# Attention with a gated feed-forward on one core: the end of the raw maxima with one transposition over 1,024 columns and three copies between partitions

## The chip, the cores and the metric

The kernel runs on one core of a Trainium2 chip. The metric is the time of one execution on the device in microseconds (us), as the median of several executions. Five engines work side by side: PE (matrix multiplications; PEld are its weight loads), DVE (vector), ACT (scalar functions), POOL (a second, slower vector engine) and SP, which here only issues transfers.

## The reference

Everything is in float32. `x` has 2,048 tokens of 448 numbers. `a` is attention with 16 heads of 28, `b` a feed-forward with 1,792 hidden units, and a gate of one number per token mixes them.

```python
q, k, v = split(x @ wqkv)                   # 16 heads of 28
p = softmax(q @ k.T * 28 ** -0.5)           # 2048 x 2048 for each head
a = (p @ v) @ wo
gate = x @ W_gate
b = (gate * (gate > 0) * (x @ W_up)) @ W_down
g = sigmoid((x * gate_w).sum(-1))
out = g * a + (1 - g) * b
```

## The kernel before

**Rounds.** Keys lie on partitions, queries along the columns. A head has 16 blocks of 128 keys; a round takes 8 of them, so 16 heads make 32 rounds of some 25 us each. In a round PE makes scores for 8 blocks of keys by 2,048 queries (`scores`, L323, and `raw_scores`, L330), maxima for the next head (`smax`, L292), a piece of the feed-forward (`gu_mm`, L716), and last the product of the probabilities with the values (`pv`, L753: 64 matmuls as PE runs them). What stands where is written by hand in the strings of `ROUNDS`, a letter for each step: s scores, r and q raw scores, d `raw_max`, m `smax`, x a feed-forward matmul, e an exponential, T the end of the raw maxima. Each engine runs its own queue in the order in which the code issues.

**Two ways to keep the exponential in bounds.** For half of the queries (column chunks 0 and 1) the maximum is known ahead and is subtracted within the matmul; ACT writes exp(score) at once (L325). For the other half (chunks 2 and 3, 1,024 queries) the scores of a round are copied out raw (L334 on ACT, L332 on DVE), one round ahead, and DVE keeps a running maximum over the 8 blocks of keys in `run(0)` and `run(1)`, each 128 partitions by 512 columns, next to each other in one tile (`raw_max`, L337; the tile is slot 8 and has the name P in the profile, as all the probability slots do).

**The end of the raw maxima** (`raw_top`, T in the strings, once in each of 31 rounds) makes one maximum for each of the 1,024 queries over the 128 partitions, all on DVE. It transposes the running maxima in blocks of 32 by 32 (L345), takes the maximum over the 32 columns of each block into `best_of`, 128 partitions by 32 (L348), copies the four groups of 32 partitions side by side on partitions 0 to 31 (`four`, L342; a copy is written as a maximum over one element), takes the maximum of the four (`square`, L351), transposes that back (L353) into a row of `rows2`, and in odd rounds also takes the maximum with the row of the round before (L356), again into `best_of`.

**What follows it.** SP writes the row to DRAM (L359, `mr_d`) and reads it back spread over all 128 partitions into the upper half of slot 8 (L366). In the next round POOL subtracts it from 8 blocks of raw scores (`raw_less`, L371, in the last round on DVE), ACT takes the exponentials (L375), and `pv` reads them. In odd rounds POOL also makes the difference of the two rows (L361). `raw_top` stands a few steps ahead of the end of a round, and `pv` comes last. Behind the end, DVE has the products of the feed-forward (L731), the copy or sum of what `pv` made (`os`, L757 and L759), and the maxima of the next round (L294), which give score banks back to PE.

**Where tiles lie.** `rows2` and `best_of` are in a pool that also holds the small tiles of `smax`; the pools with V, the first K and Q and the probability slots lie behind it.

Of the kernel before, what the change touches and what calls it, by code (L numbers as in the profile page):

```python
# [9 lines left out]
F32 = mybir.dt.float32  # L10
# [9 lines left out]
P = 128  # L20
# [109 lines left out]
def gated_mix_kernel(ctx, tc, x, wq, wo, wgu, wd, out):  # L130
    nc = tc.nc
# [5 lines left out]
    keep = ctx.enter_context(tc.tile_pool(name="keep", bufs=1))  # L137
# [88 lines left out]
    def slot(k):  # L226
        if k not in slots:
            slots[k] = p_slot((0, 1, 2, 3, 5, 6, 7, 4, 8)[k], f"P_{k}")
        return slots[k]
# [14 lines left out]
    def run(a, n=1):  # L244
        return slot(8)[:, a:a + n].rearrange("p a t -> p (a t)")
# [3 lines left out]

    rows2 = keep.tile([32, 2, 32], F32, name="rows2")  # L250
    row_a, row_b = rows2[:, 0], rows2[:, 1]
    best_of = keep.tile([P, 32], F32, name="best_of")

    Q = {}

# [83 lines left out]
    def raw_top(r):  # L339

        def copy(o, i):
            nc.vector.tensor_reduce(o, i.rearrange("p (a b) -> p a b", b=1), axis=AX.X, op=OP.max)  # L342

        for a in range(2):
            nc.vector.transpose(run(a), run(a))  # L345
        best, small = best_of, run(0)
        four, square = small[:32, :128].rearrange("p (a b) -> p a b", a=4), small[:32, 128:160]
        nc.vector.tensor_reduce(best, run(0, 2).rearrange("p (b i) -> p b i", i=32), axis=AX.X, op=OP.max)  # L348
        for a in range(4):
            copy(four[:, a], best[32 * a:32 * a + 32])  # L350
        nc.vector.tensor_reduce(square, four.rearrange("p a b -> p b a"), axis=AX.X, op=OP.max)  # L351
        row = row_b if r % 2 else row_a
        nc.vector.transpose(row, square)  # L353
        if r % 2:
            row = best_of[:32]
            nc.vector.tensor_reduce(row, rows2.rearrange("p a b -> p b a"), axis=AX.X, op=OP.max)  # L356

        def send():
            nc.sync.dma_start(mr_d[r], row)  # L359
            if r % 2:  # L360
                nc.gpsimd.tensor_tensor(row_a, row_a, row, op=OP.subtract)  # L361

        return send
# [469 lines left out]
    for r, order in enumerate(ROUNDS):  # L833
# [22 lines left out]
        for n, o in enumerate(steps):  # L856
# [3 lines left out]
            b = int(o[1]) if o[1:] else None  # L860
# [17 lines left out]
            elif o == "T":  # L878
                assert not new and not tops
                send = raw_top(r + 1)  # L880
                if not behind:
                    send()
# [50 lines left out]
        if not topped:  # L933
            raw_top(r + 1)()
# [214 lines left out]
```

## Time and profile before

| | |
|---|---|
| median of 3 executions | 1149.65 us (1149.62 to 1153.59) |
| the profiled execution | 1148.84 us, its span 1147.1 us |
| busy PE, PEld | 1142.2 us, 821.9 us |
| busy DVE, ACT, POOL | 919.6, 869.6, 705.6 us |
| granted clock of PE | 1.000 |

The span runs from the first to the last instruction of the profiled execution. In the views, a row of a group gives line, engine, operation, what is written from what is read, the shape and the count, then busy time and the mean of one in ns, then the idle time of the engine before it and who ended that. A row of a timeline gives start and duration in us, then the same; a bracket holds the idle time ahead and its releaser. "b" is the whole of PSUM, whose eight banks take what PE makes. Releasers are inferred: of several events that an instruction could wait for, the one named is the last that came.

### The profile page before, as it was taken

How to read it: one execution, taken by the hardware profiler on the slowest of the kernel's cores; microseconds unless marked ns; L12 is line 12 of the kernel's file. 1: busy time of each engine (PE TensorE's matmuls, PEld its weight loads, DVE VectorE, ACT ScalarE, POOL GpSimd, SP SyncE). 2: the span in 40 equal slices, each digit the busy share in tenths (PEclk: the TensorE clock that was granted, in tenths of full speed). 3: DMA queues.
4: the chain of work that ended last, by engine and by line, in shares of the span. 5: the costliest groups of instructions: out<-in, count | busy, mean ns of one | idle time of the engine just before them, and what ended most of it. 6: DMA issues, size and time to landing. Idle time of an engine off the chain costs nothing.

```text
span 1147.1 us, 18485 instructions
## 1 busy us (share of the span) xinstructions
PE 1142.2 (100%) x6188; PEld 821.9 (72%) x6188; DVE 919.6 (80%) x1615; ACT 869.6 (76%) x1544; POOL 705.6 (62%) x426
## 2 busy tenths in 40 slices
PE   9999999999999999999999999999999999999998
PEld 6888866666666666666666666666666666999997
DVE  6487488888899999999889999999999866544342
ACT  5311789999989999999989989999988977422221
POOL 5333368999987777878767877787887770000000
PEclk9999999999999999999999999999999999999999
DMA  9957855655664344543644354456433374654332
GB/s 315 349 193 267 310 186 183 219 195 178 204 201 144 127 153 167 176 144 125 228 145 145 115 163 153 154 175 200 140 124 121 115 252 166 209 169 131 103 106 79
DMA packets 74796, 201.50 MB, mean 176 GB/s; under 512 B 17130, under 2 KB 23746, under 8 KB 70274
## 3 DMA queue, kind: packets, MB, share of 16 engines
q1 hardware_dynamic: 67292, 171.89, 46.1%
q0 software_dynamic: 6976, 27.93, 6.7%
q8 instruction: 49, 0.80, 0.3%
q10 hardware_dynamic: 432, 0.49, 0.1%
q14 instruction: 47, 0.39, 0.1%
HBM read 139.63 MB, written 61.17 MB: 175 GB/s over the span
## 4 chain that ended last, share of the span: by engine, by line
PE 100%; DVE 0%; issue 0%
PE b L716 24%; PE b L753 20%; PE b L1053 12%; PE b L323 11%; PE b L292 11%; PE b L330 10%; PE b L524 6%; PE b L542 3%; PE b L1012 3%; PE b L572 0%; PE b L306 0%; PE b L513 0%; PE b L518 0%; DVE y L1059 0%; PE b L517 0%; DVE V L568 0%
## 5 line engine op out<-in xcount | busy, mean ns | idle before, releaser
L716 PE MATMUL b<-X,wg 128*128 128x512 f32 (+1 forms) x1232 | 389.7, 395 | 0.0
L294 DVE TENSOR_REDUCE mx<-b 128x1 f32<-128x512 f32 x528 | 339.2, 679 | 17.2 <-PE b L292 16.7
L371 POOL TENSOR_TENSOR P<-P,P 128x1024 f32<-128x1024 f32 x120 | 284.5, 2417 | 66.0 <-DMA P<-mr_d 41.3
L325 ACT ACTIVATE P<-b 128x512 f32<-128x512 f32 x528 | 301.1, 638 | 31.6 <-PE b L323 30.7
L371 POOL TENSOR_TENSOR V<-V,P 128x1024 f32<-128x1024 f32 x120 | 284.4, 2415 | 52.8 <-DMA P<-mr_d 38.1
L716 PEld LDWEIGHTS b<-X,wg 128*128 128x128 f32 (+1 forms) x1232 | 218.9, 187 | 56.7 <-issue 12.9
L337 DVE TENSOR_TENSOR P<-b,P 128x512 f32<-128x512 f32 x402 | 254.7, 681 | 1.8 <-ACT V L334 0.6
L753 PE MATMUL b<-P,v 128*32 128x512 f32 x1536 | 226.1, 594 | 0.0
L323 PE MATMUL b<-Q,K 128*128 128x512 f32 x528 | 199.3, 393 | 0.0
L292 PE MATMUL b<-K,Q 128*128 128x512 f32 x528 | 198.2, 392 | 0.0
L330 PE MATMUL b<-Q,K 128*128 128x512 f32 x496 | 184.7, 391 | 0.0
L753 PEld LDWEIGHTS b<-P,v 128*32 128x32 f32 x1536 | 60.1, 110 | 144.6 <-issue 138.4
L334 ACT ACTIVATE V<-b 128x512 f32<-128x512 f32 x239 | 137.9, 650 | 8.4 <-PE b L330 6.4
L1053 PE MATMUL b<-WD,hh 128*128 128x448 f32 x672 | 137.7, 365 | 0.0
L1053 PEld LDWEIGHTS b<-WD,hh 128*128 128x128 f32 x672 | 126.1, 188 | 10.2 <-DVE hh L189 0.2
L375 ACT ACTIVATE V<-V 128x1024 f32<-128x1024 f32 x128 | 129.4, 1113 | 1.3 <-POOL V L371 1.3
L334 ACT ACTIVATE P<-b 128x512 f32<-128x512 f32 x221 | 126.9, 645 | 3.7 <-PE b L330 1.7
L323 PEld LDWEIGHTS b<-Q,K 128*128 128x128 f32 x528 | 99.1, 188 | 30.5 <-DVE rl L731 6.7
L375 ACT ACTIVATE P<-P 128x1024 f32<-128x1024 f32 x120 | 118.1, 1071 | 0.0
L183 ACT ACTIVATE hh<-hr 128x512 fp32r<-128x512 f32 x52 | 32.8, 632 | 111.9 <-PE b L1053 111.7
L292 PEld LDWEIGHTS b<-K,Q 128*128 128x128 f32 x528 | 98.9, 188 | 20.9 <-DVE rl L731 0.8
L753 PE MATMUL b<-V,v 128*32 128x512 f32 x512 | 113.2, 594 | 0.0
(104 smaller groups left out, 1043.9 us busy)
## 6 DMA issues: line engine op xcount, KB each, us to landing
wg<-wgs_d SPq DMA_DIRECT2D x42, 896.0 KB
P<-mr_d SPq DMA_DIRECT2D x31, 512.0 KB
K<-qk_d SPq DMA_DIRECT2D x64, 224.0 KB
Q<-qk_d SPq DMA_DIRECT2D x64, 224.0 KB
h_d<-rl SPq DMA_DIRECT2D x56, 256.0 KB
hr<-h_d SPq DMA_DIRECT2D x52, 256.0 KB
wgs_d<-wg SPq DMA_DIRECT2D x14, 896.0 KB
qk_d<-st POOLq DMA_DIRECT2D x21, 512.0 KB, 5.5
```

Of the source, the lines that this page charges most:

```text
L292: nc.tensor.matmul(ps, Q[h][:, u * P:(u + 1) * P], K[h % 3][:, c * TB:(c + 1) * TB], start=True, stop=True)
L294: nc.vector.tensor_reduce(MX[h][:, k:k + 1], ps, axis=AX.X, op=OP.max)
L323: nc.tensor.matmul(ps, K[h % 3][:, kt * P:(kt + 1) * P], Q[h][:, j * TB:(j + 1) * TB], start=True, stop=True)
L325: nc.scalar.activation(prob(i, j), ps, AF.Exp, scale=SCALE)
L330: nc.tensor.matmul(ps, K[h % 3][:, kt * P:(kt + 1) * P], Q[h][:, j * TB:(j + 1) * TB], start=True, stop=True)
L334: nc.scalar.activation(prob(i, j), ps, AF.Copy)
L337: nc.vector.tensor_tensor(run(j - 2), ps, run(j - 2) if i % 8 > 1 else prob(i - 1, j), op=OP.max)
L371: engine.tensor_tensor(own, own, top(), op=OP.subtract)
L375: nc.scalar.activation(own, own, AF.Exp, scale=SCALE)
L716: nc.tensor.matmul(ps, WS[i][rows, s, a], xf(i // NF, b)[rows], start=(n == 0), stop=(n == NT - 1))
L753: nc.tensor.matmul(po[32 * j:32 * j + 32], VH[h][:, i % NK], prob(i, j), start=(i == i0), stop=(i == i0 + ni - 1))
L1053: nc.tensor.matmul(ACC[i // NF][t][:, :D], HH[i][:, a, t * P:(t + 1) * P], WD[:, f, b], start=(f == 0 and n == 0), stop=(f == NF - 1 and n ...
```

## The change

The two transpositions of 512 columns become one of 1,024 over `run(0, 2)`, which is the same memory. `best_of` grows from 32 to 128 columns, and `four` now lies in it, on partitions 0 to 31; the maxima of those partitions are already in its first 32 columns, so the first of the four copies is not needed. `square` is now in the first 32 columns of `run(0)`. In odd rounds the last maximum goes to the first 32 columns of `best_of`, as before. In the changed kernel the lines from L345 on have a number lower by one.

```diff
-    best_of = keep.tile([P, 32], F32, name="best_of")
+    best_of = keep.tile([P, 4 * 32], F32, name="best_of")
...
-        for a in range(2):
-            nc.vector.transpose(run(a), run(a))
-        best, small = best_of, run(0)
-        four, square = small[:32, :128].rearrange("p (a b) -> p a b", a=4), small[:32, 128:160]
+        nc.vector.transpose(run(0, 2), run(0, 2))
+        four, square = best_of[:32].rearrange("p (a b) -> p a b", a=4), run(0)[:32, :32]
+        best = best_of[:, :32]
         nc.vector.tensor_reduce(best, run(0, 2).rearrange("p (b i) -> p b i", i=32), axis=AX.X, op=OP.max)
-        for a in range(4):
+        for a in range(1, 4):
             copy(four[:, a], best[32 * a:32 * a + 32])
         nc.vector.tensor_reduce(square, four.rearrange("p a b -> p b a"), axis=AX.X, op=OP.max)
         row = row_b if r % 2 else row_a
         nc.vector.transpose(row, square)
         if r % 2:
-            row = best_of[:32]
+            row = best_of[:32, :32]
```

On DVE, the first end of the raw maxima, before (P_1234 is slot 8, in brackets whose events an instruction waits for):

```order
L345 STREAM_TRANSPOSE P_1234<-P_1234 128x512 [waits DVE_49] x2
L348 TENSOR_REDUCE best_of<-P_1234 128x32 [waits DVE_49]
L342 TENSOR_REDUCE P_1234<-best_of 32x32 [waits DVE_49]
L342 TENSOR_REDUCE P_1234<-best_of 32x32 x3
L351 TENSOR_REDUCE P_1234<-P_1234 32x32 [waits DVE_49]
L353 STREAM_TRANSPOSE rows_172<-P_1234 32x32 [waits DVE_49]
L356 TENSOR_REDUCE best_of<-rows_172 32x32 [waits DVE_49]
```

The same place now:

```order
L344 STREAM_TRANSPOSE P_1234<-P_1234 128x1024 [waits DVE_49]
L347 TENSOR_REDUCE best_of<-P_1234 128x32 [waits DVE_49]
L342 TENSOR_REDUCE best_of<-best_of 32x32 [waits DVE_49]
L342 TENSOR_REDUCE best_of<-best_of 32x32 x2
L350 TENSOR_REDUCE P_1234<-best_of 32x32 [waits DVE_49]
L352 STREAM_TRANSPOSE rows_172<-P_1234 32x32 [waits DVE_49]
L355 TENSOR_REDUCE best_of<-rows_172 32x32 [waits DVE_49]
```

A transposition and a copy are gone; every instruction that is left waits for the same engines as before, and the instructions of PE, ACT, POOL and SP stand in the same order in both kernels.

## The prediction

> **What bounds the kernel now.** I read the page first: who is busy, and who is on the chain that ended last.
>
> ```profile
> span 1147.1 us, 18485 instructions
> PE 1142.2 (100%) x6188; PEld 821.9 (72%) x6188; DVE 919.6 (80%) x1615; ACT 869.6 (76%) x1544; POOL 705.6 (62%) x426
> PE 100%; DVE 0%; issue 0%
> ```
>
> The chain is made of matmuls alone. A busy PE is not yet a full one, because the ends of matmuls are modelled, so I looked next at starts, in the timeline of PE around one end of the raw maxima. Columns are start, duration, engine, line, operation, count.
>
> ```profile
> 520.17 0.40 PE L292 MATMUL b<-K,Q 128*128 128x512 f32 x1
> 520.40 0.85 PE L716 MATMUL b<-X,wg 128*128 128x512 f32 x3
> 521.09 0.61 PE L292 MATMUL b<-K,Q 128*128 128x512 f32 x2
> 521.54 0.39 PE L716 MATMUL b<-X,wg 128*128 128x512 f32 x1
> 521.77 0.39 PE L292 MATMUL b<-K,Q 128*128 128x512 f32 x1
> 522.09 0.73 PE L716 MATMUL b<-X,wg 64*128 64x512 f32 x4
> 522.74 7.07 PE L753 MATMUL b<-P,v 128*32 128x512 f32 x64
> 529.75 0.27 PE L306 MATMUL b<-ident,m 128*8 128x128 f32 x1
> 529.78 0.71 PE L292 MATMUL b<-K,Q 128*128 128x512 f32 x2
> ```
>
> One start to the next is 0.23 us (520.17 to 520.40, then three in 0.69, then two in 0.45): a matmul over 512 columns starts as soon as the one ahead has streamed in. No start waits for another engine here, and the 64 matmuls of `pv` fill 522.74 to 529.75. So PE sets the time and is never kept waiting in this stretch; whatever another engine saves is worth nothing unless PE waits for it elsewhere.
>
> The same moment on DVE, in its timeline:
>
> ```profile
> 521.33 0.68 DVE L337 TENSOR_TENSOR P<-b,P 128x512 f32<-128x512 f32 x1
> 521.93 1.29 DVE L345 STREAM_TRANSPOSE P<-P 128x512 f32<-128x512 f32 x2
> 523.26 1.22 DVE L348 TENSOR_REDUCE best_of<-P 128x32 f32<-128x1024 f32 x1
> 524.51 0.74 DVE L342 TENSOR_REDUCE P<-best_of 32x32 f32<-32x32 f32 x4
> 525.28 0.37 DVE L351 TENSOR_REDUCE P<-P 32x32 f32<-32x128 f32 x1
> 525.68 0.20 DVE L353 STREAM_TRANSPOSE rows<-P 32x32 f32<-32x32 f32 x1
> 525.92 0.21 DVE L356 TENSOR_REDUCE best_of<-rows 32x32 f32<-32x64 f32 x1
> 526.06 1.86 DVE L294 TENSOR_REDUCE mx<-b 128x1 f32<-128x512 f32 x3
> 528.46 1.29 DVE L731 TENSOR_TENSOR rl<-b,rl 128x512 f32<-128x512 f32 x2 [0.31 <-ACT rl L728]
> 529.88 0.69 DVE L757 COPY os<-b 128x512 f32<-128x512 f32 x1
> 539.27 0.68 DVE L294 TENSOR_REDUCE mx<-b 128x1 f32<-128x512 f32 x1
> ```
>
> The whole end, L345 to L356, takes 4.20 us (521.93 to 526.13) and lies almost entirely under the 7.0 us of `pv`, in which PE needs nothing that stands on DVE behind the end.
>
> **The change part by part.** How often each operation runs, and the rows nearest to the new one, from the groups of DVE with shapes kept apart (busy us, mean ns; then idle before):
>
> ```profile
> L345 DVE STREAM_TRANSPOSE P<-P 128x512 f32<-128x512 f32 x62 | 40.1, 687 | 0.0
> L371 DVE TENSOR_TENSOR V<-V,P 128x1024 f32<-128x1024 f32 x8 | 9.2, 1219 | 0.0
> L353 DVE STREAM_TRANSPOSE rows<-P 32x32 f32<-32x32 f32 x31 | 6.2, 199 | 1.1
> ```
>
> *One transposition for two.* No transposition of 1,024 columns is in the trace. From 32 columns in 199 ns to 512 in 687 ns is 488 / 480 = 1.02 ns a column, so 1,024 would take 687 + 512 × 1.02 = 1.21 us; other operations over 1,024 columns take 1.22 (L348, L371). The two together took 1.29 from first start to last end, since the second starts 0.60 after the first. I take 1.22: a saving of 0.07 us. Bounds: 1.37 (two full durations of 687 ns end to end, 0.08 lost) on one side and 1.21 (0.08 saved) on the other.
>
> *One copy fewer.* Four copies take 0.74 with 175 ns for the last, so they are (0.74 − 0.175) / 3 = 0.19 us apart; one goes: 0.19. The copy that goes took partitions 0 to 31 to themselves; in its place the maxima are left where the reduction of L348 wrote them. Bounds: 0 (the first copy's start was all waiting that the next copy inherits) and 0.19.
>
> *Other addresses of four and square.* L351 still reads 128 values 32 apart on 32 partitions, now from best_of: 0.37 as before, no change. best_of is 384 bytes longer, so tiles behind it lie 384 bytes higher. The trace has the same operation on tiles in different places, and POOL, which reads two of them, shows no difference:
>
> ```profile
> L371 POOL TENSOR_TENSOR P<-P,P 128x1024 f32<-128x1024 f32 x120 | 284.5, 2417 | 66.0 <-DMA P<-mr_d 41.3 <-DVE mx L294 11.3 <-DVE V L332 9.6
> L371 POOL TENSOR_TENSOR V<-V,P 128x1024 f32<-128x1024 f32 x120 | 284.4, 2415 | 52.8 <-DMA P<-mr_d 38.1 <-ACT P L334 7.5 <-ACT P L325 3.9
> ```
>
> 2417 against 2415 ns: I take nothing for the move.
>
> *Sum on DVE:* 0.07 + 0.19 = 0.26 us in each of 31 ends, 31 × 0.26 = 8.1 us of DVE's 919.6 (between −0.08 and 0.27 each, −2.5 to 8.4 in all). The end takes 3.94 us instead of 4.20.
>
> *What of it is on the path: nothing on PE directly.* Its cover is `pv`. If that were gone, the 8.1 us would be the most that could come back. What comes earlier by 0.26 us is the row of maxima that SP sends out and spreads again, and the subtractions of POOL behind it. How often POOL waits for that, from the list of waits (us in total, times, longest):
>
> ```profile
> POOL P L371 <- DMA P<-mr_d: 41.3, 7, 8.2
> POOL V L371 <- DMA P<-mr_d: 38.1, 8, 7.2
> ```
>
> In 7 + 8 = 15 of 31 rounds the block of subtractions would start 0.26 earlier; ACT's exponentials follow, then `pv`. Whether PE sees it stands in the account of line 753, what its weight loads waited for (us, times):
>
> ```profile
>   DVE P L345: 4.7, 15
>   ACT P L325: 0.7, 2
>   ACT P L375: 0.7, 2
>   ACT V L375: 0.7, 1
> ```
>
> PE's loads waited 0.7 + 0.7 = 1.4 us for exponentials (L375) in the whole run. That bounds this route: 0 to 1.4 us gained, and I take 0, because only three waits stand behind it. The change adds no wait: L348 waited for both transpositions, and waits for the one that replaces them. No instruction of PE, ACT, POOL or SP is added, dropped or moved, so no queue has a longer wait in it.
>
> The sum on the path is 0: the profiled execution, 1148.84 with its span of 1147.1 and 1.7 around it, would be 1148.8 again. It lies 0.8 under the median of the runs, 1149.65. **I forecast 1149.5 us.** A measurement of this kernel can tell about 0.5%, 5.7 us, from no change.
>
> **The rivals.**
>
> *A, slower: PE does wait for the first of the two transpositions.* The row "DVE P L345: 4.7, 15" says that `pv`'s first weight load was released by L345, in 15 rounds, and the clock fits: the first transposition ends at 521.93 + 0.69 = 522.62, and `pv` starts at 522.74. If what releases it is the transposition, it must now wait for all 1,024 columns, 1.22 − 0.69 = 0.53 us later: 15 × 0.53 = 8.0 us, so 1149.65 + 8.0 = 1157.6. It decides from 0.38 us a round on (5.7 / 15). The Trainium skill (Perfetto Trace Analysis, § Optimizing Scalar/DVE Operations) speaks for this side: where DVE is not saturated but makes bubbles on other engines, breaking instructions up may let work complete sooner; the change does the opposite. Against it stand the weight loads themselves, in a round where L345 is named and in the next one, where it is not:
>
> ```profile
> 522.74 0.16 PEld L753 LDWEIGHTS b<-P,v 128*32 128x32 f32 x8 [0.36 <-DVE P L345]
> 550.59 0.11 PEld L753 LDWEIGHTS b<-P,v 128*32 128x32 f32 x2 [0.36 <-issue]
> 547.17 1.30 DVE L345 STREAM_TRANSPOSE P<-P 128x512 f32<-128x512 f32 x2
> ```
>
> The gap is the same 0.36 us at 550.59, 2.1 us after both transpositions had ended (548.47). So the gap belongs to the change of tile shape, and L345 is only the event that came last beside it. `pv` reads neither run nor best_of. By that rule the time would be 1157.6, by these rows 1149.5. Chance 2%.
>
> *B, faster: DVE is the bound.* PE's full rows could hide slack. The Trainium skill (Perfetto Trace Analysis, § Identifying the Most-Contended Engine) says not to judge PE by matmul busy time but by its weight loads; these are at 72%, under DVE's 80%, and by that rule DVE would be the engine to relieve. If all of DVE's saving came through, 1149.65 − 8.1 = 1141.5. Against it: the starts 0.23 us apart, and DVE itself, which sits waiting for PE after the end in other rounds:
>
> ```profile
> 557.80 0.69 DVE L759 TENSOR_TENSOR os<-b,os 128x512 f32<-128x512 f32 x1 [3.65 <-PE b L753]
> ```
>
> What DVE saves ahead of this wait only lengthens it. The trace disagrees with the rule here: weight loads run under matmuls and have idle time that PE does not. Chance 2%.
>
> *C, slower: the transposition grows faster than its columns.* At twice the pair's time, 2.58 instead of 1.29, an end would take 2.58 − 1.29 − 0.19 = 1.1 us more. The room for it: DVE idles 0.31 (L731) after the end, plus small gaps up to 0.13 (529.75 to 529.88), and then its hand-over to PE has about 0.37 to spare: L294 at 539.27 ends at 539.95, and the next matmul that scores into its bank starts at 540.32.
>
> ```profile
> 540.32 0.39 PE L323 MATMUL b<-Q,K 128*128 128x512 f32 x1
> ```
>
> That is 0.31 + 0.13 + 0.37 = 0.8 us. Beyond it each us is paid once a round: (1.1 − 0.8) × 31 = 9 us, 1159. It decides from 0.8 + 0.18 = 1.0 us of growth on. The slope of 1.02 ns a column, steady from 32 to 512, speaks against it. Chance 2%.
>
> That the change does not do what it says is hardly possible: the operations are named one by one.
>
> **How the numbers follow.** No effect 94%, A 2%, B 2%, C 2%. Faster by over 0.5% is B, 0.02; slower is A and C, 0.04; within is 0.94. The range takes the first case alone. Below 1149.65: the 1.4 us of waits for exponentials and the 0.8 between the profiled execution and the median, 1147.4. Above: the runs of before reach 1153.59, 4.0 over the median; half of that and the same 0.8 give 1152.4.
>
> **What would show it.** Right: one L344 a round at about 1.22 us, three copies in 0.55, an end of about 3.94; matmul starts still 0.23 apart; DVE's busy time about 8 us less, its idle before os longer, POOL's wait for the spread shorter by up to 4 us, PE's row unchanged. A would show in `pv` starting 0.5 us later after the last 64-row matmul than 522.09 to 522.74; C in an L344 over 2 us. The forecast is wrong if the span moves by 5.7 us, or if PE shows gaps between starts that it doesn't have now.

## The result, and the profile after

The changed kernel takes 1157.47 us (median of 6 executions, 1156.37 to 1159.38) against 1149.70 before (six executions; three of them gave the 1149.65 further up): ratio 1.0069, 95% interval 1.0058 to 1.0080. It is slower by 7.8 us, outside the stated range. That is almost to the digit the time of rival A; the experiments below show that rival A's mechanism is wrong all the same.

The head of the page of the changed kernel (in its profiled execution, 1159.02 us):

```profile
span 1157.2 us, 18423 instructions
PE 1152.4 (100%) x6188; PEld 822.6 (71%) x6188; DVE 917.3 (79%) x1553; ACT 874.6 (76%) x1544; POOL 705.8 (61%) x426
PE 100%; DVE 0%; issue 0%
```

PE is busy for 100% of the span, as before, with as many matmuls, and yet 10.2 us longer. So PE does the same work more slowly and its share does not show it. The share of the weight loads does not show it either, 72% before and 71% now. The Trainium skill (Perfetto Trace Analysis, § Identifying the Most-Contended Engine) says that matmul busy time is no good measure of how close a kernel is to its roofline, the limit set by the hardware; these two pages of the profile agree with it, 100% in both.

The end of the raw maxima on DVE, in the timeline of the changed kernel:

```profile
527.22 1.25 DVE L344 STREAM_TRANSPOSE P<-P 128x1024 f32<-128x1024 f32 x1
528.50 1.22 DVE L347 TENSOR_REDUCE best_of<-P 128x32 f32<-128x1024 f32 x1
529.76 0.56 DVE L342 TENSOR_REDUCE best_of<-best_of 32x32 f32<-32x32 f32 x3
530.35 0.39 DVE L350 TENSOR_REDUCE P<-best_of 32x32 f32<-32x128 f32 x1
530.77 0.20 DVE L352 STREAM_TRANSPOSE rows<-P 32x32 f32<-32x32 f32 x1
531.00 0.21 DVE L355 TENSOR_REDUCE best_of<-rows 32x32 f32<-32x64 f32 x1
```

It takes 3.99 us (527.22 to 531.21) instead of 4.20. The edit does on DVE nearly what was forecast. Next, rival A's place: the last feed-forward matmuls of that round on PE, and the first weight load of `pv`.

```profile
527.20 0.73 PE L715 MATMUL b<-X,wg 64*128 64x512 f32 x4
527.86 7.07 PE L752 MATMUL b<-P,v 128*32 128x512 f32 x64
```

```profile
527.86 0.16 PEld L752 LDWEIGHTS b<-P,v 128*32 128x32 f32 x8 [0.36 <-issue]
```

`pv` starts 0.66 us after the 64-row matmuls, and before it was 0.65 (522.09 to 522.74); the gap ahead of the load is the same 0.36, and no longer has DVE's name on it. The long transposition runs until 528.47, 0.6 us into `pv`. PE does not wait for it.

Where the time goes shows in the starts of `pv` along the chain that ended last (start, length, engine, line, matmuls). Before, at the first round, at rounds 19 to 23, and at the last:

```profile
151.36 7.00 PE b L753 x64
...
654.91 7.00 PE b L753 x64
680.61 7.01 PE b L753 x64
705.95 7.00 PE b L753 x64
731.64 7.00 PE b L753 x64
757.00 7.00 PE b L753 x64
...
959.27 7.00 PE b L753 x64
```

After:

```profile
153.60 7.00 PE b L752 x64
...
661.38 7.00 PE b L752 x64
687.04 7.00 PE b L752 x64
712.70 7.00 PE b L752 x64
738.64 7.00 PE b L752 x64
764.30 7.00 PE b L752 x64
...
968.62 7.00 PE b L752 x64
```

Each difference between two rows is a round. Rounds 20 to 23 took 25.70, 25.34, 25.69 and 25.36 us before and take 25.66, 25.66, 25.94 and 25.66 now: round 20 is unchanged, the three others are 0.25 to 0.32 longer. `pv` itself is 7.00 in both. From first to last `pv` it is 807.91 against 815.02, 7.1 of the 10.1 us by which this profiled span is longer (1157.2 against 1147.1). Another 2.2 us lie ahead of the first `pv`: some 1.0 of them in its 462 steps from matmul to matmul, which average 230.0 ns against 227.8, and the rest is of a size by which this stretch differs between kernels of one time (the first `pv` starts at 152.32 us in experiment 2, which takes as long as before).

Inside a slow round, the same eleven matmuls on PE, before and after (the first, second and last):

```profile
531.25 0.39 PE L292 MATMUL b<-K,Q 128*128 128x512 f32 x1
531.48 0.39 PE L323 MATMUL b<-Q,K 128*128 128x512 f32 x1
...
533.52 0.39 PE L323 MATMUL b<-Q,K 128*128 128x512 f32 x1
```

```profile
536.38 0.40 PE L292 MATMUL b<-K,Q 128*128 128x512 f32 x1
536.61 0.40 PE L323 MATMUL b<-Q,K 128*128 128x512 f32 x1
...
538.71 0.40 PE L323 MATMUL b<-Q,K 128*128 128x512 f32 x1
```

Ten steps take 2.27 us before and 2.33 after: 227 ns a matmul against 233. There is no hole in PE's row; the steps are a little longer.

What sets round 20 apart are the K and Q that it reads. Head h uses the K and Q number h modulo 3. Round 20 is the first of head 10, with the second K and Q for its scores and the third for the maxima of head 11. Rounds 21 to 23 read, beside others, the first K and Q (for the maxima of head 12, in round 23 for its raw scores). Through the whole trace, rounds 2, 8, 14, 20 and 26 alone do without the first K and Q, and their steps (from each matmul's start to the next, where that lies between 218 and 250 ns) average 227.4 to 228.3 ns; the other rounds average 229.9 to 231.7. Before, the averages of all rounds lie between 226.8 and 229.6 without that division: round 20 had 228.7 and has 228.2 now, round 22 had 228.7 and has 231.7. The first K and Q lie behind best_of, and the second and third ahead of it. In the kernel before as it is built, all K, Q and wg (the gate and up weights) and x start at 192 modulo 256 bytes of a partition (the remainder when the start is divided by 256); the 384 bytes that best_of has grown by put the first K and Q at 64, and leave the others.

### The profile page after: what moved, and what is told of

The parts are those of the page before. It is cut to its first block, busy times and chain, and to the rows that moved or that the text cites. A ratio compares the mean times of both kernels' runs of the same rounds, so it can differ in the third digit from the quotient of the medians.

```text
span 1157.2 us, 18423 instructions
## 1 busy us (share of the span) xinstructions
PE 1152.4 (100%) x6188; PEld 822.6 (71%) x6188; DVE 917.3 (79%) x1553; ACT 874.6 (76%) x1544; POOL 705.8 (61%) x426
## 4 chain that ended last, share of the span: by engine, by line
PE 100%; DVE 0%; issue 0%
PE b L715 24%; PE b L752 19%; PE b L1052 12%; PE b L323 11%; PE b L292 11%; PE b L330 10%; PE b L523 6%; PE b L541 3%; PE b L1011 3%; PE b L571 0%; PE b L306 0%; PE b L512 0%; PE b L517 0%; DVE y L1058 0%; PE b L516 0%; DVE V L567 0%
## 5 line engine op out<-in xcount | busy, mean ns | idle before, releaser
L715 PE MATMUL b<-X,wg 128*128 128x512 f32 (+1 forms) x1232 | 392.9, 398 | 0.0
L325 ACT ACTIVATE P<-b 128x512 f32<-128x512 f32 x528 | 297.6, 627 | 32.9 <-PE b L323 31.9
L715 PEld LDWEIGHTS b<-X,wg 128*128 128x128 f32 (+1 forms) x1232 | 219.2, 188 | 60.3 <-issue 12.8
L292 PE MATMUL b<-K,Q 128*128 128x512 f32 x528 | 199.4, 394 | 0.0
L334 ACT ACTIVATE P<-b 128x512 f32<-128x512 f32 x221 | 124.8, 621 | 4.4 <-PE b L330 2.2
L292 PEld LDWEIGHTS b<-K,Q 128*128 128x128 f32 x528 | 99.0, 188 | 22.0 <-DVE rl L730 0.8
```

The costliest lines, as they stand in the source:

```text
L292: nc.tensor.matmul(ps, Q[h][:, u * P:(u + 1) * P], K[h % 3][:, c * TB:(c + 1) * TB], start=True, stop=True)
L325: nc.scalar.activation(prob(i, j), ps, AF.Exp, scale=SCALE)
L334: nc.scalar.activation(prob(i, j), ps, AF.Copy)
L715: nc.tensor.matmul(ps, WS[i][rows, s, a], xf(i // NF, b)[rows], start=(n == 0), stop=(n == NT - 1))
```

## The experiments

Two theories. *Place*: PE's matmuls are slower where the operands that it reads start at different places modulo some number of bytes. *Length*: rival A. Times of before in each group of four are from the same chip.

**1. Only the place.** All instructions of before.

```diff
-    best_of = keep.tile([P, 32], F32, name="best_of")
+    best_of = keep.tile([P, 4 * 32], F32, name="best_of")[:, :32]
```

> The kernel before with best_of allocated 128 columns wide and only its first 32 used: every instruction as before, but the tiles behind best_of lie 384 bytes higher, as in the changed kernel. Theory 'place' (the first K and Q, which move against the second and third K and Q, x and the weights, make PE's matmuls 231 ns apart instead of 227 in all rounds that read them): 1156 to 1159.5 us, and the slow rounds are the same ones. Theory 'length' (rival A, PE waits for one long transposition): 1149.7, as there are two short ones.

Measured: 1157.41 us against 1149.07, ratio 1.0070 (1.0055 to 1.0085). `pv` starts at rounds 19 to 23:

```profile
660.83 7.00 PE b L753 x64
686.49 7.00 PE b L753 x64
712.15 7.00 PE b L753 x64
738.09 7.00 PE b L753 x64
763.76 7.00 PE b L753 x64
```

Rounds of 25.66, 25.66, 25.94 and 25.67: those of the changed kernel, with the old operations. The whole loss is there without the edit.

**2. The change, 512 bytes higher.**

```diff
-    best_of = keep.tile([P, 4 * 32], F32, name="best_of")
+    best_of = keep.tile([P, 5 * 32], F32, name="best_of")[:, :4 * 32]
```

> The changed kernel with best_of 160 columns wide instead of 128, of which 128 are used: the tiles behind it lie 512 bytes higher than before instead of 384. Theory 'place': if what counts repeats every 512 bytes or less, PE is back at 227 ns and the time at 1149.4 to 1149.8. Theory 'length': 1157, the operations are those of the change.

Measured: 1149.02 against 1149.07, ratio 1.0000 (0.9990 to 1.0009). The same rounds, then its page's row of engines:

```profile
655.85 7.00 PE b L752 x64
681.49 7.01 PE b L752 x64
706.83 7.00 PE b L752 x64
732.49 7.01 PE b L752 x64
757.85 7.00 PE b L752 x64
```

```profile
PE 1142.5 (100%) x6188; PEld 821.9 (72%) x6188; DVE 914.3 (80%) x1553; ACT 869.4 (76%) x1544; POOL 704.7 (61%) x426
```

25.64, 25.34, 25.66 and 25.36: the old rounds, with the new operations. DVE is 5.3 us less busy (914.3 against 919.6), and the time is the same. This is what the edit itself does.

**3. One transposition, nothing moved.**

```diff
-        for a in range(2):
-            nc.vector.transpose(run(a), run(a))
+        nc.vector.transpose(run(0, 2), run(0, 2))
```

> The kernel before with the two transpositions made one, and nothing else: no tile moves, four copies. Theory 'place': 1149.4 to 1149.8. Theory 'length': 1157, since it is the transposition that PE would wait for.

Measured: 1149.36 against 1149.07, ratio 1.0003 (0.9993 to 1.0013). The length of the transposition costs PE nothing; *length* falls.

**4. 256 bytes.** As 1, with 96 columns.

> The kernel before with best_of 96 columns wide, of which 32 are used: tiles behind it 256 bytes higher. Theory 'place': 1149.7 if what counts repeats every 256 bytes (x lies 256 bytes off a multiple of 512 from the rest already and does no harm), 1156 to 1159 if it repeats only every 512. Theory 'length': 1149.7.

Measured: 1149.19, ratio 0.9999 (0.9990 to 1.0009). What counts repeats every 256 bytes.

**5 and 6. Which tiles.** V, the first K and Q, and the probability slots had all moved. In 5 the pads leave V where it was, move the first K and Q by 128 bytes and the slots by 256; in 6 they move V by 128 and the rest by 256.

```diff
     V = vp.tile([P, G, 4, NK, 32], F32, name="V")
+    vp.tile([P, 32], F32, name="pad_1")
...
     QB = [(keep if r else vp).tile([P, 4, TB], F32R, name=f"Q{r}", tag=f"Q{r}", bufs=1) for r in range(3)]
+    vp.tile([P, 32], F32, name="pad_2")
```

```diff
+    vp.tile([P, 32], F32, name="pad_1")
     V = vp.tile([P, G, 4, NK, 32], F32, name="V")
+    vp.tile([P, 32], F32, name="pad_2")
```

> The kernel before with a pad of 128 bytes ahead of the first K and one behind the first Q: these two lie 128 bytes higher, the probability slots and all behind them 256, everything else where it was. Theory 'K and Q' (PE's own reads of the first K and Q against its other operands): 1155 to 1159.5. Rival 'V and slots' (what ACT, DVE and POOL write in V and the probability slots collides with PE's reads): 1149.1.

> The kernel before with a pad of 128 bytes ahead of V and one behind it: V lies 128 bytes higher, the first K and Q and all behind them 256. Theory 'K and Q': 1149.1. Rival 'V and slots': above 1152.

Measured: 1157.15 (ratio 1.0068, 1.0053 to 1.0083) with the first K and Q moved, 1148.93 (1.0001, 0.9992 to 1.0011) with V, against 1148.96. Moving the first K and Q brings the whole loss while V and the slots stay where they were modulo 256, so it is not what the other engines write there. With the slow rounds, which are those in which PE reads these two tiles, it is PE's reads of K and Q.

**7 and 8. By itself or against the others.** In 7 all tiles on the left lie 128 bytes higher (the first edit), in 8 (both edits) the tiles on the right, wg among them, also move, by 128 downwards, so that all agree again.

```diff
-    const.tile([P, 16], F32, name="pad")
+    const.tile([P, 48], F32, name="pad")
```

```diff
     assert m == len(MAXIMA), m
+    fe.tile([P, 32], F32, name="pad_fe")
```

> The kernel before with all tiles on the left, x, all K and Q, V and the slots, 128 bytes higher, and the gate and up weights (wg), v and the other tiles on the right where they were. If the start of a tile modulo 256 counts by itself (192 good, 64 bad): 1160 or more, as all K, Q and x are at 64. If it counts against the other operands' starts: between 1149 and 1160, as only pairs with wg differ, which are 1,232 of the matmuls, 40 of 100 in attention.

> The kernel before with all tiles on the left 128 bytes higher and those on the right 128 bytes lower: all operands of PE in attention start at 64 modulo 256 instead of 192. If the start counts by itself: 1160 or more. If only differences between operands count: 1149.1.

Measured: 1164.15 (ratio 1.0129, 1.0114 to 1.0144) in 7, and 1149.22 (0.9999, 0.9990 to 1.0009) in 8. 7 went beyond the 1160 that "against the others" was given, and 8 decides for it: all operands at 64 modulo 256 are as good as all at 192. In 7 round 20 is slow too, since wg is read in every round:

```profile
663.38 7.00 PE b L753 x64
689.33 7.00 PE b L753 x64
715.05 7.00 PE b L753 x64
741.00 7.00 PE b L753 x64
```

25.95, 25.72 and 25.95 for rounds 20 to 22, against 25.70, 25.34 and 25.69 before.

Behind the last `pv` PE runs 22 feed-forward matmuls with nothing between them, before and in 7:

```profile
966.21 5.29 PE L716 MATMUL b<-X,wg 128*128 128x512 f32 x22
```

```profile
978.44 5.39 PE L716 MATMUL b<-X,wg 128*128 128x512 f32 x22
```

In 7 every x that streams through PE here starts at 64 modulo 256 and every weight at 192. Streams agree with streams and weights with weights, and yet the row is 0.10 us longer: the last 16 steps average 233.4 ns, against 226.9 before. A stream that starts elsewhere than the weights is enough for the loss.

**9 to 12. How far, and which operand.** As 1, with 40, 48 and 80 columns (32, 64 and 192 bytes), and the first Q alone by 128 bytes.

```diff
+    vp.tile([P, 32], F32, name="pad_1")
     QB = [(keep if r else vp).tile([P, 4, TB], F32R, name=f"Q{r}", tag=f"Q{r}", bufs=1) for r in range(3)]
+    vp.tile([P, 32], F32, name="pad_2")
```

> The kernel before with best_of 40 columns wide, 32 used: tiles behind it 32 bytes higher, so the first K and Q start 32 off the others modulo 256. If any difference but a multiple of 256 costs the same: 1157. If the cost follows the size of the difference or sets in at 64 or 128: 1149.0.

> As the last, with 48 columns: 64 bytes. If any difference but a multiple of 256 costs the same: 1157. If what counts repeats every 64 bytes: 1149.0, which 128 has already shown to be slow, so that would speak for 128 as a special case. If the cost grows with the difference: about 1153.

> With 80 columns: 192 bytes, which is 64 short of 256. If the cost depends on the distance to the next multiple of 256, the same time as with 64 bytes; if any difference costs the same, 1157.

> The kernel before with the first Q alone 128 bytes higher and the first K where it was. PE takes the first Q as moving operand of scores and as weights of maxima, each time with the first K as the other. If what a matmul streams and the weights that are loaded for the next one collide: some 1154 to 1157, near the 1157.2 of both moved. If it is the two operands of the same product: 1155 to 1158, more than with both moved by the same amount. If K alone matters: 1149.0.

Measured, against 1149.26: 1160.47 with 32 bytes (ratio 1.0099, 1.0084 to 1.0114), 1157.62 with 64 (1.0074, 1.0059 to 1.0089), 1157.20 with 192 (1.0073, 1.0057 to 1.0090), 1153.98 with Q alone (1.0044, 1.0029 to 1.0059). In the rounds these differences cost the same: from first to last `pv` it is 814.4 us with 32 bytes, 814.5 with 64 and 814.1 with 192, against 807.9 before. So the cost does not grow with the difference. The 3 us more with 32 bytes, which no expectation had, lie mostly behind the last `pv`, which takes 190.5 us there against 188.7 with 64 bytes and 187.8 with 192; what costs them was not followed up. Q alone costs 4.7 us, a little over half of K and Q together, and comes out just under the 1154 to 1157 that was expected where a stream meets the next weights.

## Why the prediction was wrong

**The step that failed** is "I take nothing for the move". It rested on POOL's subtractions, 2417 against 2415 ns for tiles in two places. Those rows could not tell: POOL is not the engine that sets the time, and both tiles started at the same place modulo 256, 192. The rows to ask were PE's, and in the kernel before all of PE's operands in scores, maxima and feed-forward start at 192 too, so its trace held no case of the other kind. The sum had bounds for its other terms, and none for this. Its size is 8.3 us (experiment 1, 1157.41 − 1149.07), and it is all of the loss. The sign that the prediction named, "matmul starts still 0.23 apart", could not have shown it: 227 and 233 ns are both 0.23.

**The sum on the path** was 0 for the edit itself, and is 0: 1149.02 against 1149.07 in experiment 2. That PE is "never kept waiting" holds in the changed kernel too. What did not hold is the conclusion that the time then can't move: a row that is full says that nothing else sets the time, and not that its own steps stay as long as they are.

**The terms on DVE.** The rows of the transposition and the copies after:

```profile
L344 DVE STREAM_TRANSPOSE P<-P 128x1024 f32<-128x1024 f32 x31 | 38.5, 1243 | 0.8
L342 DVE TENSOR_REDUCE best_of<-best_of 32x32 f32<-32x32 f32 x93 | 16.3, 175 | 1.9
```

1.24 us against the 1.22 that was taken, which the bounds (1.21 to 1.37) held, so 0.05 saved in place of 0.07; the copies went from 0.74 to 0.56, 0.18 for 0.19. The end is 0.21 shorter, for 0.26; 31 × 0.21 = 6.5 for the forecast 8.1, and in DVE's busy time 2.3 in the changed kernel (917.3) and 5.3 in experiment 2.

**Rival A** forecast 1157.6 and the measurement is 1157.47, by accident. Its mechanism is refuted three times: `pv` starts no later after the matmuls ahead of it, one transposition alone costs nothing (1149.36), and two short ones are as slow where the tiles lie higher (1157.41). The argument from the 0.36 us gap was sound. **Rival B** falls with experiment 2, where 5.3 us less on DVE bring nothing. **Rival C** falls with the 1.24 us.

**Which reads collide.** Experiment 5 moved the first K and Q together, so the two operands of any one product agreed as before, and yet cost 8.2 us; so it is between operands of matmuls that follow each other. In experiment 7 no stream of a round starts at another place than the next one's, and it is the slowest kernel of all; so the collision does not need two streams. What fits both is a stream that meets the weights of a neighbour. The loads do run under the matmul ahead: in the changed kernel one of L292 starts at 526.66 us, together with a matmul of L715, and its own matmul at 526.88. **Still open** is why it is so, and whether two streams that start at different places cost something besides.

## What to carry to other kernels

A buffer that grows moves all that is allocated behind it; on a kernel whose PE row is full, compare the starts of PE's operands modulo 256 before and after, or pad until the growth is a multiple of 256 bytes, as experiment 2 does (512 for 384). A change of one or two per cent that leaves every engine's share nearly as it was is looked for in the step from start to start of the bounding engine, round by round, against the tiles that each round reads. And a forecast that comes out on the number is no proof of its mechanism: run the mechanism alone, and the rest without it.

## What the runs showed of the hardware

The matmuls of scores, maxima and feed-forward, 512 columns each, follow each other at 227 ns where the operands of neighbours start at the same place modulo 256 bytes of a partition, and at some 230 to 232 on the average of a round where some don't (32, 64, 128, 192 and 384 bytes apart; 256 and 512 are free). The place itself does not matter, 1149.22 us with all at 64. `pv` took 7.00 us in each kernel, but is no test: its four narrow weights, 128 bytes each, start at 192 and 64 by turns in all of them. The Trainium skill (SBUF — State Buffer, § Who interferes with whom) says that PE never waits on anyone and gives it two independent read ports, for the moving operand and for the weight load. No run here shows PE slowed by another engine's writes (moving V costs nothing, 1148.93 us in experiment 6). But the two reads of PE are not independent here: where stream and weights start at different places, 22 matmuls took 5.39 us instead of 5.29, and the measurement decides.
